# Handing ScalarE's exps lasting buffers, and raising the floor of TensorE work in the attention ramp

## The chip, the core and the metric

The kernel runs on one core of a Trainium2 chip. Its engines have queues of their own, each executed in order: TensorE (PE in the profile, its weight loads PEld), VectorE (DVE), ScalarE (ACT), GpSimd (POOL) and SyncE (SP, which here only issues DMAs). They are tied together by semaphores. The metric is the device time of one execution in microseconds; before the change it is 1373.56 us, the median of three runs (1373.54, 1373.56 and 1381.38).

## What is computed

Two pairs of layers act on x, 2048 rows of 512 values. The first layer of a pair is a spectral filter: layer norm, two-dimensional real FFT, product with a complex filter, inverse FFT, added to x. The second is attention with 32 query heads of 16 channels and one key and value head that all of them share.

```python
def _A_ref(x, w_r, w_i):
    X = rfft2(x.astype(float32), axes=(-2, -1))
    X = X * (w_r + 1j * w_i)
    return irfft2(X, s=(S, D), axes=(-2, -1)).astype(bfloat16)

def _B_ref(x, wq, wk, wv, wo):              # H = 32, Dh = 16
    q = (x @ wq).reshape(B, S, H, Dh).transpose(0, 2, 1, 3)
    k, v = x @ wk, x @ wv
    scores = einsum("bhqd,bkd->bhqk", q, k) * (Dh ** -0.5)
    p = softmax(scores, axis=-1)
    o = einsum("bhqk,bkd->bhqd", p, v)
    return o.transpose(0, 2, 1, 3).reshape(B, S, H * Dh) @ wo

x = x + _A_ref(_layernorm(x), w_r, w_i)
x = x + _B_ref(_layernorm(x), wq, wk, wv, wo)
x = x + _A_ref(_layernorm(x), w_r, w_i)
x = x + _B_ref(_layernorm(x), wq, wk, wv, wo)
```

## The kernel before

The Fourier transforms are matrix products on TensorE with butterflies on VectorE around them; x stays in SBUF for the whole kernel. The attention of a layer is cut into 32 blocks (four groups of 512 queries, four groups of eight heads, two parities), each of 16 key chunks by four heads. The unit of work is one head, one key chunk of 128 keys and 512 queries: a score matmul that uses 32 rows of the array (L1212, four of them side by side), an exponential, and a matmul with V that uses 32 columns (L1234).

The exponentials are shared out between two paths. ScalarE takes two units in one instruction (`exp`, L1217), from one of the two PSUM slots `sa` to a bf16 tile `e2`. VectorE takes one unit in one instruction (`p1`, L1224), which computes an approximation by way of the bit pattern; three shifted copies of it are summed in the matmul with V, two of them made by GpSimd (L1228) or VectorE. Over both layers ScalarE has 1252 such instructions and VectorE 1592.

The order on every engine is written out beforehand, by a planner in Python (`Plan`) that runs while the program is built. It keeps a clock for each engine and a price for each operation (an exp 908 ns, a `p1` 600 ns, a round of matmuls 220 ns), picks step by step what could start first and emits the instruction. The chip follows these orders without change; only the waits between engines decide when a thing starts. Three of the planner's rules matter here:

- `live` and `bufs` (L158, L159): at most `E_BUFS = 8` exps may hold a tile whose matmuls with V are not yet emitted. `do_pv` (L537) counts the readers of a tile down and lowers `live` at the last.
- `fill` (L437): before TensorE takes something up, dummy matmuls on zeros (`dummy`, L939; its two forms are at L941 and L945) are put in while the columns streamed in the last `WIN = 3413` ns are fewer than `warm`. Where the gap is too short for a dummy, it is put in all the same, ahead of the useful work, if they are fewer than `force`.
- The ramp (L439): for 20,000 ns from the point where VectorE joins the attention (`dve_on`, set when the last values of V are evacuated by L1190), `fill` uses `RAMP_WARM` and `RAMP_FORCE` in place of `WARM` and `FORCE`.

The `e2` tiles come from a tile pool with 13 buffers (`t2`, L930). Four kinds of data live there: an exp's result, the transposed x at the front of a spectral layer (`tr_evac`, L998, read by `mm1`, L1006), and the inverse transform's result and its sums (`inv_evac`, L1115, and `radix_v`, L1120). A new tile takes a buffer when all accesses to the previous one are over: the instruction that writes first waits for the engines that read and for the engine that wrote. For an exp these are TensorE (readers) and ScalarE itself (writer), beside TensorE again for the scores.

Of the kernel before, what the change touches and what calls it, by code (L numbers as in the profile page):

```python
# [8 lines left out]
ACT = mybir.ActivationFunctionType  # L9
ALU = mybir.AluOpType  # L10
P = 128
BF = mybir.dt.bfloat16
# [6 lines left out]
NC = 4  # L19
# [3 lines left out]
SCALE = DH ** -0.5  # L23
# [37 lines left out]
def radix4(nc, sd, x, half, o, piece):  # L61

    s, d = sd[:, 0], sd[:, 1]
    tt = nc.vector.tensor_tensor
    if piece == 0:
        tt(out=s, in0=x[:, 0:2, :], in1=x[:, 2:4, :], op=ALU.add)
    elif piece == 1:
        tt(out=d, in0=x[:, 0:2, :], in1=x[:, 2:4, :], op=ALU.subtract)
    elif piece == 2:
        tt(out=o[:, 0, :], in0=s[:, 0, :], in1=s[:, 1, :], op=ALU.add)  # L70
        tt(out=o[:, 2, :], in0=s[:, 0, :], in1=s[:, 1, :], op=ALU.subtract)
    else:
        o = o.rearrange("p j (i f) -> p (j i) f", i=2)
        a, b = (d[:, i].rearrange("p (i f) -> p i f", i=2) for i in range(2))
        tt(out=o[:, 2:8:5], in0=a, in1=b[:, ::-1], op=ALU.subtract)
        tt(out=o[:, 6:2:-3], in0=a, in1=b[:, ::-1], op=ALU.add)
# [34 lines left out]
class Plan:  # L111
# [17 lines left out]
    WARM = 3500.0  # L129
    FORCE = 3150.0  # L130
    RAMP = 20000.0
    RAMP_WARM = 4200.0
    RAMP_FORCE = 3900.0
    HOLD = 200.0
    NB = 4
    TIER = 500.0
# [400 lines left out]
    def do_pv(self, start, sel):  # L537
        self.fill(start, "col")
        at = self.at
        start = max(start, self.t["PE"] + (0.0 if self.mode == "col" else self.PE_SW))  # L540
        end = start + self.MM
        for s in sel:
            e = next(x for x in self.pv if x[1:5] == s[1:5] and x[5] is s[5] and x[6:8] == s[6:8])
            self.pv.remove(e)
            _, _, b, h, kc, tile, j, p, ref = e
            if b not in self.acc_of:
                self.acc_of[b] = self.grab("b", "acc")
            first = (b, h) not in at.begun
            at.begun.add((b, h))
            stop = self.made(b, h) and not any(x[2] == b and x[3] == h for x in self.pv)  # L550
            self.em.pv(self.acc_of[b], h, kc, tile, j, p, first, stop)
            ref[0] -= 1
            if ref[0] == 0:
                self.live[ref[1]] -= 1
            if self.made(b) and not any(x[2] == b for x in self.pv):
                at.done(b, self.acc_of.pop(b), end)
        self.mode = "col"
        self.hist.append((start, 128.0 * len(sel)))
        self.t["PE"] = end
# [99 lines left out]
class Layer:  # L659
# [11 lines left out]
    def __init__(self, plan, em, first, last):  # L671
        self.plan, self.em, self.first, self.last = plan, em, first, last
        self.next = None
        self.at = Attn(plan, em, self)
        self.rs = {}
        self.Pk, self.G, self.FT, self.W, self.Dz, self.IT, self.UT, self.V, self.sb, self.xn = ({} for _ in range(10))
        self.mm1_done = {}
        self.g_done = {}
        self.stat = {}
        self.gate = []  # L680
        self.sd_of = {}
# [194 lines left out]
class Emit:  # L876


    def __init__(self, ctx, tc, ins, out):
        nc = self.nc = tc.nc  # L880
        A_x, self.w_r, self.w_i, B_wq, B_wk, B_wv, B_wo = ins
        mk = lambda nm, b=1, **kw: ctx.enter_context(tc.tile_pool(name=nm, bufs=b, **kw))
        const = mk("const")
        psum = mk("psum", space=bass.MemoryType.PSUM)
        self.pool = mk("work")
        self.sa = [psum.tile([P, 2, 512], F32, name=f"sa{i}") for i in range(2)]
        self.b = [psum.tile([P, 512], F32, name=f"b{i}") for i in range(Plan.NB)]
        nc.scalar.preload_act_table_set("natural_log_exp_and_others")
        self.x = const.tile([P, R, T, 512], BF, name="x_sb")
        xv = A_x.flatten_outer_dims().rearrange("(r p t) d -> p r t d", r=R, p=P, t=T)  # L890
        ht = host_tables()
        self.dram = {k: nc.inline_tensor(v, name=f"const_{k}").ap() for k, v in ht.items()}
        tabs = {name: const.tile(list(ht[name].shape), BF, name=f"tab_{name}") for name in ("ident", "PH", "PS")}
        self.ident, self.PH, self.PS = tabs["ident"], tabs["PH"], tabs["PS"]
        nc.sync.dma_start(out=self.x[:, :, 0], in_=xv[:, :, 0])
        nc.scalar.dma_start(out=self.ident, in_=self.dram["ident"])
        nc.scalar.dma_start(out=self.PH, in_=self.dram["PH"])
        for t in range(1, T):
            nc.sync.dma_start(out=self.x[:, :, t], in_=xv[:, :, t])
        self.wq = const.tile([P, NC, D], BF, name="wq")  # L900
        self.wk = const.tile([P, NC, DH], BF, name="wk")
        self.wk8 = const.tile([P, NC, P], BF, name="wk8")
        self.part = const.tile([P, 2], F32, name="part")
        self.wv = const.tile([P, NC, DH], BF, name="wv")
        self.WO = const.tile([P, 4, D], BF, name="WO")
        self.eps = const.tile([P, 1], F32, name="eps")
        self.zero = const.tile([P, 512], BF, name="zero")
        self.KA = const.tile([P, S], BF, name="KA")
        self.KB = const.tile([P, S], BF, name="KB")
        self.warm = const.tile([P, 2, 16], U16, name="warm")  # L910
        nc.vector.memset(self.zero, 0.0)
        nc.vector.memset(self.eps, EPS)
        nc.gpsimd.memset(self.warm, 0)
        self.key = const.tile([P, 1], F32, name="key")
        self.pw = phase_weights()
        self.VS = [const.tile([P, NT, 32], BF, name=f"vs{i}") for i in range(1 + K_PH)]
        for i, v in enumerate(self.VS):
            nc.gpsimd.memset(v, 1.0 if i == 0 else self.pw[i - 1])
        nc.gpsimd.int64_add(self.warm[:, 1].bitcast(U64), self.warm[:, 0].bitcast(U64), 0)
        half = (np.arange(P)[:, None] // DH % 2 == np.arange(2)).astype(np.float32)  # L920
        self.w_dma = [(self.PS, self.dram["PS"]), (self.wq, B_wq.rearrange("(c p) j -> p c j", p=P)),
                      (self.wk, B_wk.rearrange("(c p) j -> p c j", p=P)), (self.wv, B_wv.rearrange("(c p) j -> p c j", p=P)),
                      (self.part, nc.inline_tensor(half, name="const_part").ap()),
                      (self.WO, B_wo.rearrange("(g p) c -> p g c", p=P))]
        self.out_v = out.flatten_outer_dims().rearrange("(r p t) d -> p r t d", r=R, p=P, t=T)
# [1 line left out]
    def t4(self, shape, dt=BF, tag="w4", bufs=17):  # L927
        return self.pool.tile([P] + list(shape), dt, name=tag, tag=tag, bufs=bufs)

    def t2(self, shape, dt=BF, bufs=13):  # L930
        return self.pool.tile([P] + list(shape), dt, name="e2", tag="e2", bufs=bufs)

    def small(self, shape, name, bufs=6):
        return self.pool.tile([P] + list(shape), F32, name=name, tag=name, bufs=bufs)
# [63 lines left out]
    def tr_evac(self, L, tiles, slot, eng):  # L998
        xt = self.t2([2, NC, P])
        src = self.ps(slot).bitcast(BF)  # L1000
        dst = xt.rearrange("p i c x -> p (i c x)")
        self.copy(eng, dst, src)
        L.xt = dict(getattr(L, "xt", {}))
        L.xt[tuple(tiles)] = xt

    def mm1(self, L, tiles, i, slot, cc):  # L1006
        xt = L.xt[tuple(tiles)]
        self.nc.tensor.matmul(self.ps(slot), lhsT=xt[:, i, cc, :], rhs=self.PH[:, cc, :], start=(cc == 0), stop=(cc == NC - 1),
                              skip_group_check=True)

    def mm1_evac(self, L, x, slot):
        t, r = x
# [102 lines left out]
    def inv_evac(self, L, t, b, j, slot, eng):  # L1115
        if (t, b) not in L.V:
            L.V[(t, b)] = self.t2([4, 256])
        self.copy(eng, L.V[(t, b)][:, 2 * j:2 * j + 2, :].rearrange("p a b -> p (a b)"), self.ps(slot))

    def radix_v(self, L, t, b, piece):  # L1120
        if t not in L.UT:
            L.UT[t] = self.t4([2, R, 256])
        if piece == 0:
            L.sd_of[(t, b)] = self.t2([2, 2, 256])
        u = L.UT[t][:, b]
        radix4(self.nc, L.sd_of[(t, b)], L.V[(t, b)], 128, u, piece)

    def y_mm(self, L, t, r, slot, s, n):
        if s == 4:
# [20 lines left out]
            self.nc.tensor.transpose(ps[:, cc, i, :], xn[:, cc * P:(cc + 1) * P], self.ident)  # L1150

    def copy(self, eng, out, in_):
        if eng == "ACT":
            self.nc.scalar.copy(out=out, in_=in_)
        else:
            self.nc.vector.tensor_copy(out=out, in_=in_)

    def trn_evac(self, L, t, j, slot, eng):
        xT = L.at.xT
# [54 lines left out]

    def exp(self, slot, us):
        e = self.t2([2, 512])
        self.nc.scalar.activation(out=e, in_=self.ps(slot), func=ACT.Exp, scale=SCALE)  # L1217
        return e

    def new_t(self):  # L1220
# [131 lines left out]
```

The softmax here doesn't subtract the row's maximum and nothing guards it: scores larger than these inputs give would overflow.

## Time and profile before

| | |
|---|---|
| median of the runs | 1373.56 us (1373.54 to 1381.38) |
| profiled execution | 1376.24 us |
| its span | 1374.4 us |
| mean granted TensorE clock | 0.991 |
| weight loads (PEld) busy | 432.2 us, 13009 instructions |
| matmuls | 12937 |
| exps (L1217) | 1252 |
| dummies at L941, L945 | 55 and 44 matmuls (the latter are four to a dummy) |

A profile row "start, duration, engine, line, operation" gives microseconds from the start of the span. A matmul's duration includes its passage through the array, so four matmuls side by side that take 0.39 us each follow the previous four after 0.22 us. ScalarE's instructions overlap too: an exp of 1.02 us can start 0.904 us after the one before. A share of busy time close to 100% says that an engine is nearly always occupied, not that it works at its peak. The clock granted to TensorE is given as a share of full speed; it changes only in steps of 3.41 us. Instructions that only wait on a semaphore (EVENT_SEMAPHORE) do not count as busy.

### The profile page before, as it was taken

How to read it: one execution, taken by the hardware profiler on the slowest of the kernel's cores; microseconds unless marked ns; L12 is line 12 of the kernel's file. 1: busy time of each engine (PE TensorE's matmuls, PEld its weight loads, DVE VectorE, ACT ScalarE, POOL GpSimd, SP SyncE). 2: the span in 40 equal slices, each digit the busy share in tenths (PEclk: the TensorE clock that was granted, in tenths of full speed). 3: DMA queues.
4: the chain of work that ended last, by engine and by line, in shares of the span. 5: the costliest groups of instructions: out<-in, count | busy, mean ns of one | idle time of the engine just before them, and what ended most of it. 6: DMA issues, size and time to landing. Idle time of an engine off the chain costs nothing.

```text
span 1374.4 us, 32527 instructions
## 1 busy us (share of the span) xinstructions
PE 1331.3 (97%) x12937; PEld 432.2 (31%) x13009; DVE 1288.9 (94%) x2286; ACT 1253.5 (91%) x1408; POOL 828.0 (60%) x810
## 2 busy tenths in 40 slices
PE   9999999999999999999999999999999999999998
PEld 5632222222223222232246322222222222222222
DVE  6985899999999999999979879999999999998998
ACT  6498899999998999999954989999999989997996
POOL 0001677757776777657720027777777767776775
PEclk9998899999999999999999999999999999999999
DMA  8100000000000000000051000000000000000000
GB/s 285 40 1 1 2 1 2 1 2 1 2 2 1 2 2 1 2 2 1 2 161 40 1 1 2 2 2 9 9 2 1 5 13 2 1 2 17 1 2 17
DMA packets 21081, 22.07 MB, mean 16 GB/s; under 512 B 2240, under 2 KB 19648, under 8 KB 20928
## 3 DMA queue, kind: packets, MB, share of 16 engines
q1 hardware_dynamic: 20640, 19.44, 4.5%
q8 instruction: 101, 1.65, 0.5%
q14 instruction: 52, 0.43, 0.1%
q10 hardware_dynamic: 288, 0.56, 0.1%
HBM read 17.89 MB, written 2.10 MB: 15 GB/s over the span
## 4 chain that ended last, share of the span: by engine, by line
PE 61%; DVE 17%; ACT 15%; issue 4%; DMA 1%; SPq 1%; POOL 1%; DVEq 0%; POOLq 0%; ACTq 0%
PE sa_65 L1212 8%; PE sa_64 L1212 8%; PE b_68 L1234 7%; PE b_69 L1234 7%; PE b_67 L1234 7%; PE b_66 L1234 5%; PE b_68 L1212 3%; PE b_69 L1212 2%; PE b_66 L1212 2%; PE b_67 L1212 2%; DVE st L959 1%; DVE x_sb L1144 1%; DVE xd L57 1%; DMA w_368<-const_FT 1%; PE b_68 L1133 1%
## 5 line engine op out<-in xcount | busy, mean ns | idle before, releaser
L1212 PEld LDWEIGHTS <-KA 32*128 32x128 bf16 x2048 | 82.7, 91 | 226.9 <-issue 220.9
L1212 PEld LDWEIGHTS <-KB 32*128 32x128 bf16 x2048 | 79.7, 91 | 234.0 <-issue 229.8
L1234 PEld LDWEIGHTS <-vs_96 128*32 128x32 bf16 x2504 | 104.2, 94 | 108.4 <-issue 99.7
L1234 PEld LDWEIGHTS <-vs_97 128*32 128x32 bf16 x1592 | 93.7, 94 | 72.1 <-issue 69.4
L1234 PEld LDWEIGHTS <-vs_98 128*32 128x32 bf16 x1592 | 71.0, 94 | 83.4 <-issue 77.8
L1234 PEld LDWEIGHTS <-vs_99 128*32 128x32 bf16 x1592 | 70.3, 94 | 78.6 <-issue 73.0
L1228 POOL INT64_ADD w_1549<-w_1548 x1 | 1.0, 1042 | 123.8 <-DVE w_1548 L1224 123.8
L1228 POOL INT64_ADD w_11726<-w_11725 x1 | 1.0, 1040 | 111.8 <-DVE w_11725 L1224 111.8
L959 DVE BATCH_NORM_STATS2 st<-x_sb 128x6 f32<-128x512 bf16 x52 | 35.6, 685 | 4.7 <-DMA x_sb<-in_A_x_dram 3.9
L1099 PEld LDWEIGHTS <-xd 128*128 128x128 bf16 x256 | 24.0, 98 | 9.3 <-DVE xd L57 4.4
L1252 DVE TENSOR_TENSOR on<-raw,rc 128x512 bf16<-128x512 f32 x32 | 21.8, 682 | 0.1
L1212 PE MATMUL sa_65<-w_903,KB 32*128 32x512 bf16 x86 | 18.2, 387 | 0.3
L1212 PE MATMUL sa_65<-w_11080,KB 32*128 32x512 bf16 x86 | 18.0, 382 | 0.3
L1212 PE MATMUL sa_64<-w_903,KA 32*128 32x512 bf16 x84 | 17.1, 392 | 1.1 <-ACT e_2850 L1217 0.2
L1212 PE MATMUL sa_65<-w_903,KA 32*128 32x512 bf16 x84 | 17.6, 394 | 0.5 <-ACT e_2505 L1217 0.2
L1212 PE MATMUL sa_64<-w_11080,KA 32*128 32x512 bf16 x84 | 16.6, 382 | 1.3 <-ACT e_13213 L1217 0.4
L1212 PE MATMUL sa_65<-w_2548,KB 32*128 32x512 bf16 x80 | 17.1, 382 | 0.9 <-ACT e_4970 L1217 0.2
L1212 PE MATMUL sa_64<-w_903,KB 32*128 32x512 bf16 x86 | 17.5, 396 | 0.3 <-ACT e_2605 L1217 0.2
L1212 PE MATMUL sa_65<-w_11080,KA 32*128 32x512 bf16 x84 | 17.1, 383 | 0.5 <-ACT e_12682 L1217 0.2
L1212 PE MATMUL sa_64<-w_11080,KB 32*128 32x512 bf16 x86 | 16.9, 383 | 0.4 <-ACT e_12782 L1217 0.2
L1212 PE MATMUL sa_65<-w_4927,KB 32*128 32x512 bf16 x80 | 16.9, 382 | 0.4 <-ACT e_6743 L1217 0.2
L1212 PE MATMUL sa_65<-w_12725,KB 32*128 32x512 bf16 x78 | 16.4, 381 | 0.4
(6372 smaller groups left out, 6569.3 us busy)
## 6 DMA issues: line engine op xcount, KB each, us to landing
it<-const_IT SPq DMA_DIRECT2D x8, 640.0 KB, 6.3
x_sb<-in_A_x_dram SPq DMA_DIRECT2D x4, 512.0 KB, 7.2
out_dram<-x_sb SPq DMA_DIRECT2D x16, 128.0 KB, 1.8
tab_PH<-const_PH ACTq DMA_DIRECT2D x1, 512.0 KB, 5.3
w_107<-const_FT SPq DMA_DIRECT2D x1, 512.0 KB, 8.9
w_112<-const_FT SPq DMA_DIRECT2D x1, 512.0 KB, 8.4
tab_PS<-const_PS SPq DMA_DIRECT2D x1, 512.0 KB, 7.8
wq<-in_B_wq_dram SPq DMA_DIRECT2D x1, 512.0 KB, 7.9
```

Of the source, the lines that this page charges most:

```text
L57: nc.vector.tensor_tensor(out=sd[:, 2 * piece:2 * piece + 2, :], in0=x[:, 0:2, :], in1=x[:, 2:4, :], op=ALU.subtract if piece else ALU.add)
L959: self.nc.vector.bn_stats(st, self.ps(slot) if slot else self.x[:, x[1], x[0], :])
L1099: self.nc.tensor.matmul(ps[:, k, :], lhsT=z, rhs=L.IT[t][:, u, w:w + 256], start=(a == 0 and i == 0), stop=(a == 1 and i == 1), skip_group ...
L1133: self.nc.tensor.matmul(self.ps(slot), lhsT=L.UT[t][:, b, r, 128 * i:128 * i + 128], rhs=self.PS[:, s, :], start=(s == 0), stop=(s == n - ...
L1144: self.nc.vector.tensor_tensor(out=x, in0=self.ps(slot), in1=x, op=ALU.add)
L1212: self.nc.tensor.matmul(o, lhsT=KX[rs, kc * P:(kc + 1) * P], rhs=at.QT[qb][rs, g, :], start=True, stop=True, skip_group_check=True)
L1228: self.nc.gpsimd.int64_add(t[p][:, 0:n].bitcast(U64), t[0][:, 0:n].bitcast(U64), DELTA[p] * FOUR)
L1234: self.nc.tensor.matmul(self.ps(slot)[32 * h:32 * h + 32, :], lhsT=V[:, kc, :], rhs=rhs, start=first, stop=last, skip_group_check=True)
L1252: self.nc.vector.tensor_tensor(out=on.rearrange("p a h d -> p h a d"), in0=raw[:, :, :, 0:16], in1=rc.unsqueeze(3).to_broadcast([P, 2, 16, ...
```

## The change

The 13 `e2` buffers become tiles that last for the whole kernel (`e2_0` to `e2_12`). `t2` hands out the oldest idle one; `free2` puts it back when the planner has emitted its last reader. `wrote` remembers for each buffer which engine last wrote it, and with which instruction; when the same engine writes it again by way of `wrote`, the dependence between these two writes is declared void. This holds for exps and for the transposed x. Buffers written for the inverse transform have their record dropped. `copy` now returns its instruction. Beside this, two of the planner's numbers are raised, `RAMP_WARM` from 4200 to 4800 and `RAMP_FORCE` from 3900 to 4300.

```diff
-    RAMP_WARM = 4200.0
-    RAMP_FORCE = 3900.0
+    RAMP_WARM = 4800.0
+    RAMP_FORCE = 4300.0
...
             if ref[0] == 0:
                 self.live[ref[1]] -= 1
+                if ref[1] == "ACT":
+                    self.em.free2(tile)
...
+        self.tc = tc
+        self.e2 = [const.tile([P, 1024], BF, name=f"e2_{i}") for i in range(13)]
+        self.idle, self.home, self.writer = list(range(13)), {}, {}
...
-    def t2(self, shape, dt=BF, bufs=13):
-        return self.pool.tile([P] + list(shape), dt, name="e2", tag="e2", bufs=bufs)
+    def t2(self, shape):
+
+
+        home = self.idle.pop(0)
+        dims = " ".join("abc"[:len(shape)])
+        view = self.e2[home].rearrange(f"p ({dims}) -> p {dims}", **dict(zip("abc", shape)))
+        self.home[id(view)] = (home, view)
+        return view
+
+    def free2(self, view):
+        self.idle.append(self.home.pop(id(view))[0])
+
+    def wrote(self, eng, view, i):
+
+
+        home = self.home[id(view)][0]
+        last = self.writer.get(home)
+        if last is not None and last[0] == eng:
+            self.tc.declare_no_dep(i.ins, last[1].ins, reason="the readers of that write waited for it")
+        self.writer[home] = (eng, i)
...
-        self.copy(eng, dst, src)
-        L.xt = dict(getattr(L, "xt", {}))
-        L.xt[tuple(tiles)] = xt
+        self.wrote(eng, xt, self.copy(eng, dst, src))
+        L.xt[tuple(tiles)] = [xt, 2 * NC]
...
+        L.xt[tuple(tiles)][1] -= 1
+        if L.xt[tuple(tiles)][1] == 0:
+            self.free2(L.xt.pop(tuple(tiles))[0])
...
         self.copy(eng, L.V[(t, b)][:, 2 * j:2 * j + 2, :].rearrange("p a b -> p (a b)"), self.ps(slot))
+        self.writer.pop(self.home[id(L.V[(t, b)])][0], None)
...
+            self.writer.pop(self.home[id(L.sd_of[(t, b)])][0], None)
...
+        if piece == 1:
+            self.free2(L.V[(t, b)])
+        if piece == 3:
+            self.free2(L.sd_of[(t, b)])
...
         e = self.t2([2, 512])
-        self.nc.scalar.activation(out=e, in_=self.ps(slot), func=ACT.Exp, scale=SCALE)
+        self.wrote("ACT", e, self.nc.scalar.activation(out=e, in_=self.ps(slot), func=ACT.Exp, scale=SCALE))
         return e
```

## The prediction

> **What bounds the kernel now.** I read the page's shares first, then the chain of work that ended last, then busy time by stretches, and then single instructions. The first two lines below are from part 1 and part 2 of the page, the third from part 4.
>
> ```profile
> PE 1331.3 (97%) x12937; PEld 432.2 (31%) x13009; DVE 1288.9 (94%) x2286; ACT 1253.5 (91%) x1408; POOL 828.0 (60%) x810
> ...
> PEclk9998899999999999999999999999999999999999
> ...
> PE 61%; DVE 17%; ACT 15%; issue 4%; DMA 1%; SPq 1%; POOL 1%; DVEq 0%; POOLq 0%; ACTq 0%
> ```
>
> Three engines are almost full, and no single one is the bound: the chain lies mostly on PE and changes over to DVE and ACT for stretches. The two long attention stretches, in busy time (columns: stretch, length, busy of PE, weight loads, DVE, ACT, POOL with instruction counts, granted clock, DMA):
>
> ```profile
> 172.00:640.00 468.00, 459.11 (x4690) 134.19 (x4715) 461.21 (x790) 455.29 (x498) 337.58 (x330) 1.00 0.01 2
> 840.00:1240.00 400.00, 392.78 (x4043) 111.66 (x4057) 394.64 (x657) 391.40 (x421) 301.25 (x290) 1.00 0.01 4
> ```
>
> There PE, DVE and ACT are each at 97 to 99%. A saving on one of them alone is worth little; it counts only where the chain passes through it. The row of granted clock above shows an 8 in the fourth and fifth slices, so I looked at those in the steps in which the clock record changes, 3.41 us:
>
> ```profile
> 122.01:125.42 3.41, 2.49 (x19) 0.78 (x18) 2.60 (x7) 3.38 (x4) 0.00 (x0) 1.00 0.02 5
> 125.42:128.83 3.41, 3.41 (x23) 0.59 (x21) 1.29 (x2) 2.10 (x3) 2.06 (x2) 0.50 0.00 0
> ...
> 135.66:139.07 3.41, 3.41 (x18) 0.64 (x17) 1.98 (x3) 0.68 (x2) 2.06 (x2) 0.50 0.00 0
> ...
> 811.50:814.91 3.41, 2.93 (x28) 0.80 (x21) 2.22 (x4) 2.54 (x4) 2.31 (x3) 1.00 0.02 7
> 814.91:818.33 3.42, 2.74 (x17) 0.74 (x17) 2.99 (x5) 2.91 (x3) 1.86 (x3) 1.00 0.00 0
> ...
> 1238.17:1241.58 3.41, 3.34 (x9) 0.81 (x9) 2.00 (x4) 1.64 (x2) 1.05 (x2) 0.50 0.11 38
> ```
>
> From 125.4 to 145.9 TensorE ran five of six such steps at half clock, just after VectorE's share of the attention begins (the "ramp" of the planner). The ramp of the second layer, 811 to 818, is the same planned work and kept the full clock. So the two are a measured pair. The last values' evacuation (L1190) opens the ramp, the second block's evacuation (L1241) closes it, in the timeline of VectorE:
>
> ```profile
> 122.05 0.23 DVE L1190 CAST vs_96<-b_69 128x64 bf16<-128x64 f32 x1
> ...
> 146.86 0.71 DVE L1241 STREAM_TRANSPOSE raw<-b_66 128x512 f32<-128x512 f32 x1
> ```
>
> ```profile
> 806.42 0.22 DVE L1190 CAST vs_96<-b_66 128x64 bf16<-128x64 f32 x1
> ...
> 824.94 0.70 DVE L1241 STREAM_TRANSPOSE raw<-b_67 128x512 f32<-128x512 f32 x1
> ```
>
> 24.8 us against 18.5 us: the half clock cost 6.3 us in the first layer and nothing in the second.
>
> **The change part by part.** *The wait on ScalarE's own write.* The instructions of the exp's line begin with
>
> ```profile
> L1217 ACTq EVENT_SEMAPHORE  x1116: 17/17/17, 84.9 to 1362.6; - x186
> ```
>
> Of 1252 exps, 1116 have a separate wait instruction ahead of them: the exp itself waits on ScalarE's semaphore and the event instruction on TensorE's. By the wait values of the program the own write waited for lies 10 to 15 ScalarE instructions back, some 10 us, so that wait is never the late one; what it costs is that the wait for the scores needs an instruction of its own. Without one (the timeline's first pair) and with one (the second), the exp follows its scores like this:
>
> ```profile
> 75.91 0.39 PE L1212 MATMUL sa_65<-w_903,KA 32*128 32x512 bf16 x2
> ...
> 76.33 1.02 ACT L1217 ACTIVATE e_954<-sa_65 128x1024 bf16<-128x1024 f32 x1
> ```
>
> ```profile
> 432.86 0.39 PE L1212 MATMUL sa_65<-w_4927,KB 32*128 32x512 bf16 x2
> ...
> 433.35 1.02 ACT L1217 ACTIVATE e_6266<-sa_65 128x1024 bf16<-128x1024 f32 x1 [4.73 <-PE sa_64 L1212]
> ```
>
> That is 0.03 us after the matmul's end without, 0.10 us with. Pairing every exp with the semaphore update of its scores gives medians of 0.023 (40 late exps) and 0.083 us (180), so 0.06 us for each exp whose scores come late. An exp that is not late gains nothing: back to back, exps start every 0.904 us with the event instruction and without. Late (scores at least 0.84 us after the previous exp's start) are 280 exps with an event instruction: 280 x 0.06 = 16.8 us is the ceiling. The floor is what the chain of waits shows: it passes from PE to ACT 12 times between 172 and 640 and 15 times between 840 and 1240, so 27 x 0.06 = 1.6 us, and a few more outside. Other chains lie close behind the shown one (PE at 98%), so I take the value near the floor: -2.0 us. It could also be zero, if each saved 0.06 us ends in a wait for DVE.
>
> *The lasting buffers.* 13 buffers before, 13 after, of the same size; the exp still waits for TensorE's last read of its buffer, in the same instruction as for its scores. The planner holds at most 8 exps at a time, so there is normally an idle one. Buffers of the transposed input, of V and of its sums come from the same 13 and have their writer forgotten, so a few dozen exps keep extra waits. No instruction is added. Zero; what hides it is that the oldest idle buffer is handed out. If none but a just-freed buffer were there, an exp would wait for a round of L1234 (0.22 us); the tight places (602 to 606 us, where x is transposed into these buffers) have a few such, under 1 us.
>
> *RAMP_WARM 4200 to 4800, RAMP_FORCE 3900 to 4300.* The planner puts dummy matmuls (L941, L945) into the ramp until that many columns lie in its window of 3413 ns, and forces them ahead of useful work below the second number. A ramp has 22 us, or 6.5 windows. The rise of 600 columns is 600/512 x 6.5 = 8 more dummies in a ramp, of which 400/512 x 6.5 = 5 are forced. Before, each ramp had 13. At full clock dummies start 0.22 us apart (6.34, 6.56, 6.77 us in the trace), so forced ones cost at most 1.1 us a ramp; PE has 0.5 to 0.7 us idle in each of the steps at 811 to 818 above, so I take half: +1.1 us for both ramps. What it may bring is the 6.3 us of the first ramp, all or nothing.
>
> [...] The step at 811 with 28 matmuls kept its clock, the one at 122 with 19 lost it; eight dummies over 6.5 windows, more at the thin ones, make up that order of difference. [...]
>
> *Sum.* -5.2 - 2.0 = -7.2 us, so 1376.24 - 7.2 = 1369.0 for the profiled execution. Its span is 1374.4 with 1.8 us around it, and it is 2.7 us above the median of the runs (1373.56). The half-clock stretch at 1238 to 1245 may be that difference: ScalarE stands idle for 5.1 us at its end, waiting for scores. I leave it as it is on both sides. Against the median: 1366.4 us.
>
> **The rivals.** *The clock is not won (0.18).* The first ramp still falls under what the clock wants. For it: I can't see the limit, only pairs of rows, and the thin time is in the waits of TensorE for VectorE, where the plan and the chip differ. Against: the second ramp is clear with today's dummies. 1373.6 - 2.0 + 1.1 to 2.0 (dummies at half clock start 0.43 us apart, as 3.30 and 3.72 us show) = 1373.
>
> *The wait is worth more (0.14).* ACT at 97% in the long stretches may be the pacing engine oftener than one chain shows. Two thirds of the ceiling, 11 us, with the ramp: 1373.6 - 5.2 - 11 = 1357.
>
> *The clock is lost in another place (0.16, the slower side).* The second ramp kept its clock with steps of PE busy 2.74 and 2.93 us, barely more than the 2.49 that lost it, and the stretch at 1238 lost it. Moving everything by some microseconds moves the thin stretches against the steps of the clock. If the second ramp is caught and the first is not saved: +6.3 + 2.0 - 2.0 = 1380. It decides once one 3.41 us step of the second ramp holds as little as the first's. More dummies there speak against; the run of 1381.38 among three of before speaks for such a loss being possible.
>
> *It doesn't do what it says.* If the event instructions stay (the readers' wait and the scores' wait not merged), only the ramp acts: 1368. This is inside the first case's spread.
>
> **How the numbers follow.** First case 0.52, 1366.4, own range 1361 to 1371; then 0.18 at 1373, 0.14 at 1357, 0.16 at 1380. The range 1355 to 1379 leaves out about half of the slower rival and the far tails. One per cent is 13.7 us, about what a measurement of this kernel tells from no change: faster than 1359.8 takes most of the third case and a little of the first, 0.16; slower than 1387.3 needs two lost ramps and more, 0.05; within it 0.79.
>
> **What would show it.** The event instructions at the exp's line fall from 1116 to well under 200, and late exps start about 0.03 us after their scores. The steps between 122 and 146 us show a clock of 1.00, and the first layer's pair of lines comes to about 18.5 us. More than 13 dummies lie in each ramp, and the second ramp is under 1 us longer. The prediction is wrong if 0.50 rows stay in the first ramp or appear in the second, or if the long stretches (172 to 640 in particular) get shorter by more than 3 us or longer by any.

## The result, and the profile after

The changed kernel takes 1359.87 us in the median of four runs (1359.69 to 1365.84), the kernel before beside it 1373.55 us (1372.03 to 1381.38): a ratio of 0.990, 95% interval 0.9854 to 0.9946. The prediction was 1366.4 us with a range of 1355 to 1379. Direction and range hold; the gain is 13.7 us where 7.2 were forecast. In a second set, five runs against 17 of before, the ratio is 0.9903 (0.9874 to 0.9932).

Every run lists its mean granted TensorE clock, and the time goes with it. In what follows "at full clock" means a mean of 0.999 or 1.000. Two executions in all (1423 us and 1631 us) had a mean clock of 0.84 and 0.65, for a reason that no run here shows, and are left out of the comparisons.

The changed kernel's page, the lines that answer to those of before (busy shares, clock row, the chain that ended last):

```profile
PE 1316.5 (97%) x12952; PEld 426.1 (31%) x13022; DVE 1283.2 (95%) x2285; ACT 1249.4 (92%) x1409; POOL 825.7 (61%) x809
...
PEclk9999999999999999999999999999999999999999
...
PE 40%; ACT 39%; DVE 16%; issue 2%; POOL 1%; DMA 1%; SPq 1%; DVEq 0%; POOLq 0%; ACTq 0%
```

The shares have hardly moved. The clock row has lost both its 8s. The chain has changed: ScalarE holds 39% of it where it held 15%. The first ramp of the changed kernel, in the steps of its own clock record (columns as before: stretch, length, PE, weight loads, DVE, ACT, POOL, clock, DMA):

```profile
120.89:124.30 3.41, 2.97 (x34) 1.23 (x32) 2.06 (x6) 3.28 (x5) 0.00 (x0) 1.00 0.02 5
124.30:127.72 3.42, 2.86 (x27) 0.74 (x23) 2.45 (x4) 2.93 (x4) 0.65 (x1) 1.00 0.00 0
127.72:131.13 3.41, 3.17 (x34) 0.64 (x26) 2.67 (x5) 2.34 (x4) 2.65 (x4) 1.00 0.00 0
131.13:134.54 3.41, 2.62 (x26) 0.82 (x26) 2.43 (x4) 2.85 (x3) 1.10 (x2) 1.00 0.00 0
```

The clock stays at 1.00. The same pair of lines as before, the last values' evacuation (now L1218) and the second block's (now L1269), in VectorE's timeline:

```profile
122.28 0.22 DVE L1218 CAST vs_109<-b_69 128x64 bf16<-128x64 f32 x1
...
141.88 0.70 DVE L1269 STREAM_TRANSPOSE raw<-b_66 128x512 f32<-128x512 f32 x1
```

19.6 us instead of 24.8. The same pair in the second layer:

```profile
796.05 0.22 DVE L1218 CAST vs_109<-b_66 128x64 bf16<-128x64 f32 x1
...
815.65 0.70 DVE L1269 STREAM_TRANSPOSE raw<-b_67 128x512 f32<-128x512 f32 x1
```

Here it is 19.6 us instead of 18.5, with the full clock on both sides. So the first ramp gained by the clock, and the second, where no clock had been lost, became 1.1 us longer. The exps now wait for their scores themselves, as two lines of the timeline show:

```profile
446.79 0.39 PE L1240 MATMUL sa_64<-w_4622,KA 32*128 32x512 bf16 x2
...
447.22 1.02 ACT L1245 ACTIVATE e_1_87<-sa_64 128x1024 bf16<-128x1024 f32 x1
```

The exp starts 0.04 us after the matmul ends (446.79 + 0.39 = 447.18), where it was 0.10 with a wait instruction between. Over the whole trace, 6 exps have a wait instruction (1116 before), and late exps start 0.023 us (median) after their scores' semaphore. Back to back, exps start 0.904 us apart, as before.

### The profile page after: what moved, and what is told of

It reads as the page before. It is cut to its first block, busy times and chain, and to the rows that moved or that the text cites. A ratio compares the mean times of both kernels' runs of the same rounds, so it can differ in the third digit from the quotient of the medians.

```text
span 1357.7 us, 31441 instructions
## 1 busy us (share of the span) xinstructions
PE 1316.5 (97%) x12952; PEld 426.1 (31%) x13022; DVE 1283.2 (95%) x2285; ACT 1249.4 (92%) x1409; POOL 825.7 (61%) x809
## 4 chain that ended last, share of the span: by engine, by line
PE 40%; ACT 39%; DVE 16%; issue 2%; POOL 1%; DMA 1%; SPq 1%; DVEq 0%; POOLq 0%; ACTq 0%
PE sa_64 L1240 5%; PE sa_65 L1240 5%; PE b_67 L1262 5%; PE b_68 L1262 5%; PE b_69 L1262 4%; ACT e_10_96 L1245 3%; ACT e_3_89 L1245 3%; ACT e_0_86 L1245 3%; ACT e_2_88 L1245 3%; ACT e_11_97 L1245 3%; ACT e_9_95 L1245 3%; ACT e_12_98 L1245 3%; ACT e_5_91 L1245 3%; ACT e_7_93 L1245 3%; ACT e_1_87 L1245 3%; ACT e_6_92 L1245 3%
## 5 line engine op out<-in xcount | busy, mean ns | idle before, releaser
L1240 PEld LDWEIGHTS <-KA 32*128 32x128 bf16 x2048 | 77.6, 91 | 220.4 <-issue 215.5
L1245 ACT ACTIVATE e_0_86<-sa_65 128x1024 bf16<-128x1024 f32 x50 | 52.2, 1043 | 7.0 <-PE sa_64 L1240 6.2
L1245 ACT ACTIVATE e_2_88<-sa_65 128x1024 bf16<-128x1024 f32 x51 | 53.0, 1039 | 1.8 <-PE sa_64 L1240 0.8
L1245 ACT ACTIVATE e_8_94<-sa_64 128x1024 bf16<-128x1024 f32 x49 | 51.2, 1044 | 2.9 <-PE sa_64 L1240 2.4
L1245 ACT ACTIVATE e_10_96<-sa_64 128x1024 bf16<-128x1024 f32 x49 | 51.0, 1040 | 3.1 <-PE sa_65 L1240 3.0
L1245 ACT ACTIVATE e_9_95<-sa_64 128x1024 bf16<-128x1024 f32 x50 | 52.0, 1040 | 0.8 <-PE b_68 L1240 0.7
L1245 ACT ACTIVATE e_4_90<-sa_65 128x1024 bf16<-128x1024 f32 x50 | 52.2, 1044 | 0.3
L1245 ACT ACTIVATE e_8_94<-sa_65 128x1024 bf16<-128x1024 f32 x49 | 51.4, 1049 | 1.1 <-PE sa_64 L1240 1.1
L1245 ACT ACTIVATE e_7_93<-sa_64 128x1024 bf16<-128x1024 f32 x49 | 51.4, 1048 | 0.9 <-PE sa_65 L1240 0.8
L1245 ACT ACTIVATE e_6_92<-sa_65 128x1024 bf16<-128x1024 f32 x48 | 50.1, 1043 | 2.1 <-PE sa_64 L1240 2.1
L1245 ACT ACTIVATE e_2_88<-sa_64 128x1024 bf16<-128x1024 f32 x47 | 48.9, 1039 | 3.3 <-PE sa_64 L1240 3.3
L1245 ACT ACTIVATE e_12_98<-sa_65 128x1024 bf16<-128x1024 f32 x49 | 51.1, 1043 | 0.7 <-PE b_67 L1240 0.4
L1245 ACT ACTIVATE e_12_98<-sa_64 128x1024 bf16<-128x1024 f32 x47 | 49.3, 1048 | 2.5 <-PE sa_65 L1240 2.1
L1245 ACT ACTIVATE e_0_86<-sa_64 128x1024 bf16<-128x1024 f32 x49 | 51.3, 1047 | 0.2
L1245 ACT ACTIVATE e_10_96<-sa_65 128x1024 bf16<-128x1024 f32 x48 | 50.4, 1050 | 0.9 <-PE sa_65 L1240 0.7
```

Source lines behind the costliest of these rows:

```text
L1240: self.nc.tensor.matmul(o, lhsT=KX[rs, kc * P:(kc + 1) * P], rhs=at.QT[qb][rs, g, :], start=True, stop=True, skip_group_check=True)
L1245: self.wrote("ACT", e, self.nc.scalar.activation(out=e, in_=self.ps(slot), func=ACT.Exp, scale=SCALE))
```

## The experiments

Three parts were to be told apart: the wait, the lasting buffers, and the two ramp numbers; the latter may act through the clock or through the order that the planner writes.

**The ramp numbers alone.** The kernel before with

```diff
-    RAMP_WARM = 4200.0
-    RAMP_FORCE = 3900.0
+    RAMP_WARM = 4800.0
+    RAMP_FORCE = 4300.0
```

> The kernel before with the two ramp numbers alone (4800 and 4300). If the clock in the first ramp is all that these numbers buy, as the prediction has it: 5 to 6 us below before, no step at half clock between 122 and 146 us, the pair of lines L1190 to second L1241 near 18.5 us, 1116 or so wait instructions still there. If the ramp numbers also make a better schedule of the rest: 10 us or more below before. If they did nothing and the whole gain is the wait: within 1 us of before.

Measured: 1366.58 us, ratio 0.9935 (0.9911 to 0.9959), 7.9 us below before (1374.51 in that set). Of the comparable runs two were at clock 1.000 (1365.0 and 1365.4) and the others at 0.998 or 0.999, up to 1366.9. The profiled one had no half clock in the first ramp, took 19.6 us for each ramp's pair of lines, and lost the clock for 3.4 us at 1230. More than the expected 5 to 6 us, so the clock is not all that the numbers buy.

**The wait alone.** The changed kernel with the ramp numbers of before:

```diff
-    RAMP_WARM = 4800.0
-    RAMP_FORCE = 4300.0
+    RAMP_WARM = 4200.0
+    RAMP_FORCE = 3900.0
```

> The changed kernel with the two ramp numbers put back to 4200 and 3900. If only the passages from PE to ACT on the shown chain count (the prediction): 2 us below before. If ScalarE paces the long stretches oftener than one chain shows: 6 to 11 us below before, spread evenly over both long stretches. The half clock in the first ramp should be seen again; if it is gone here too, it was a matter of the ramp's timing against the clock's steps and not of the number of dummies.

Measured: 1368.71 us, ratio 0.9940 (0.9907 to 0.9974), 5.8 us below before. Every engine's order is that of before, so blocks can be compared one by one. From the second to the thirtieth block's evacuation it takes 517.2 us (before 519.7), from the 34th to the 54th 359.0 us (360.5). The gain is spread over both long stretches, 2.5 and 1.4 us. The chain of this run:

```profile
PE 49%; ACT 33%; DVE 14%; issue 2%; DMA 1%; SPq 1%; POOL 0%; DVEq 0%; POOLq 0%; ACTq 0%
```

Without the wait ScalarE holds 33% of the chain, and with the ramp numbers alone 19%, so the shift is the wait's doing and not the ramp's. In this profiled run the half clock in the first ramp is there again, as the stretch shows:

```profile
122.00:146.00 24.00, 22.72 (x125) 4.28 (x123) 13.44 (x25) 12.97 (x14) 8.21 (x8) 0.57 0.00 1
```

It also lost the clock in the second ramp, from 807.3 to 810.7 us, where the profile of before, with the same order, had kept it. But three of its seven runs kept the clock (0.999 or 1.000), and those took 1362.0 to 1362.2 us. Losing the ramp's clock differs from run to run; it is not a fixed property of an order. At equal mean clock (0.985, 0.991 and 0.992) the four other runs lie 4.8 to 5.6 us below the runs of before.

**The lasting buffers alone.** The changed kernel, ramp numbers and buffers included, with the declaration left out:

```diff
         if last is not None and last[0] == eng:
-            self.tc.declare_no_dep(i.ins, last[1].ins, reason="the readers of that write waited for it")
+            pass
```

> The changed kernel, lasting buffers and ramp numbers as changed, but the dependence on ScalarE's own last write kept. If the lasting buffers cost and bring nothing by themselves: the same time as the ramp numbers alone, within 1 us, with over 1100 wait instructions back. If it is the order in which buffers are handed out that matters: near the changed kernel's 1360 us.

Measured: 1366.80 us (0.9947, 0.9925 to 0.9968); at clock 1.000, 1364.5 to 1365.5 us, the same as the ramp numbers alone. 1113 wait instructions are back and late exps again start 0.083 us after their scores. Lasting buffers bring nothing and cost nothing by themselves; they are what lets the declaration be made. The profiled run lost the clock in the second ramp, 802 to 816 us, which the profile of before had not shown.

**Half of the waits.** The changed kernel with the declaration for the six odd buffers only:

```diff
-        if last is not None and last[0] == eng:
+        if last is not None and last[0] == eng and home % 2:
```

> The changed kernel with the wait on the own last write kept for the seven even buffers and voided for the six odd ones, so that about half of the wait instructions are back; the order on every engine is that of the changed kernel. If every late exp passes its 0.06 us on, wherever it lies, the undisturbed time lies half way between the changed kernel (1359.7) and the ramp numbers alone (1365.0): about 1362.4. If only a few places on one chain pay, it lies at one end or the other, within 1 us.

The exps' line has

```profile
L1245 ACTq EVENT_SEMAPHORE  x611: 17/17/17, 85.2 to 1348.6; - x153
```

Measured: median 1367.21 us of 12 runs (0.9940, 0.9916 to 0.9964); the five at full clock took 1361.9 to 1363.8 us, their middle 1362.8. 611 of 1113 waits are 55%, and 55% of the way from 1359.8 to 1365.2 is 1362.8. So about half of the waits cost about half of the time. The other seven had clocks of 0.985 to 0.994: in the changed kernel's own order on every engine the clock is lost in many runs.

**Ramp numbers 4600 and 4100.** The changed kernel with

```diff
-    RAMP_WARM = 4800.0
-    RAMP_FORCE = 4300.0
+    RAMP_WARM = 4600.0
+    RAMP_FORCE = 4100.0
```

> The changed kernel with ramp numbers 4600 and 4100. Theory 1, each added dummy costs a little: fewer dummies, so 0.2 to 1 us below the changed kernel's 1359.7 when the clock holds, but the half clock comes back in some runs. Theory 2, the numbers only tip the planner's choices and the rest of the order changes by chance: the undisturbed time goes with the length of the order as planned, which is 2 us shorter than the changed kernel's, so about 1357.5.

Measured: 1364.27 us (0.9936, 0.9914 to 0.9958). None of 12 runs kept the full clock; the six best were at 0.994 or 0.995, 1361.5 to 1363.2 us. The profiled one was at half clock from 125 to 139, and its pair of lines to the second block ends at 146.1 us against 141.9 in the changed kernel. Taking these 4.2 us off the 1361.8 of that run gives an estimate of 1357.6 for this order at full clock, which is what theory 2 says; it wasn't seen directly. Theory 1 would have it at 1358.7 to 1359.5.

**Ramp numbers 5400 and 4900.** The same two lines with these values.

> The changed kernel with ramp numbers 5400 and 4900, 26 more dummies. Theory 1, forced dummies at 0.22 us each, half of them on the path: about 3 us above 1359.7, no half clock anywhere in the ramps. Theory 2, the order as planned is 11 us longer: about 1370, no half clock either.

Measured: 1371.65 us (0.9979, 0.9960 to 0.9997). At clock 0.999 or 1.000, 1369.9 to 1371.8 us. The ramps kept their clock in the profiled run, which lost it elsewhere, at 594 to 604 us. Theory 2: the order as planned is 11 us longer, and so is the time. The 26 more dummies would be 5.7 us at 0.22 us each. In the ramps the pair of lines took 21.6 us each time, 2.0 us more than in the changed kernel; the rest of the loss lies elsewhere, in the order that the planner wrote.

**True prices for the planner.** The changed kernel with

```diff
-    PE_LAT = {"ACT": 252.0, "DVE": 205.0, "POOL": 252.0}
+    PE_LAT = {"ACT": 192.0, "DVE": 205.0, "POOL": 252.0}
...
-    ACT_EXP = 908.0
+    ACT_EXP = 904.0
```

> The changed kernel with the planner's prices brought to what the traces show: an exp 904 ns instead of 908, and from scores to exp 192 ns instead of 252, the 60 ns that the wait instruction took. If the planner gains from true prices: 1357 to 1358 (its order is 1.7 us shorter). If its order differs only by chance: anywhere from 1355 to 1366, and no better where the thin stretches lose the clock.

Measured: 1364.31 us (0.9943, 0.9918 to 0.9969), at full clock 1363.5 to 1365.5 us. It is slower than the changed kernel although its order is 1.7 us shorter by the planner's clock. A miss: truer prices made a plan that the chip falls behind by more. Why is open.

**The changed kernel again.** No edit.

> The changed kernel as it is, in more runs, since a median of four may be a lucky draw: the kernel with half of the waits has the same order and held the full clock in 5 of 12 runs. If the changed kernel keeps the clock by itself: nearly all runs within 0.5 us of 1359.7. If it is the same draw as for that order: about half of the runs at 1359.7, the others 1 to 8 us above with a clock of 0.985 to 0.998, and a median of 1360 to 1365.

Measured: five comparable runs, 1359.6, 1360.0, 1360.1, 1361.5 and 1365.0 us, the first four at 0.999 or 1.000. With the four of the first measurement that is seven of nine at full clock, with a median of 1360.0. The half-waits kernel, with the same order, had five of twelve. So the first median was no lucky draw, but the clock isn't safe in this order.

**Force 4000.** The changed kernel with

```diff
-    RAMP_WARM = 4800.0
-    RAMP_FORCE = 4300.0
+    RAMP_WARM = 4400.0
+    RAMP_FORCE = 4000.0
```

> The changed kernel with ramp numbers 4400 and 4000. By the planner's own books the first number changes nothing here (every gap in a ramp is too short for a dummy that would wait its turn); the second alone sets the order. This order is 2.4 us shorter than the changed kernel's, and its thinnest 3413 ns of the ramps hold 3107 columns against 2816. If the undisturbed time goes with the length of the order: 1357.4. If the clock goes with the thinnest stretch: more runs undisturbed than the changed kernel has; if it doesn't, as few or fewer.

Measured: 1358.15 us, ratio to before 0.9890 (0.9863 to 0.9917). Four of six runs kept the full clock, at 1357.7 to 1358.3 us; the others had 0.995 and 0.997 (1363.3 and 1361.5). At full clock this is 1.8 us below the changed kernel; 2.4 were expected from the length of the order. The clock was not kept oftener (four of six runs, seven of nine for the changed kernel), so nothing here says that the thinnest stretch of the plan sets the odds. It is the fastest version of this study; the runs of this and of the changed kernel in the same set (medians 1358.15 and 1360.1) overlap, so only the comparison at full clock tells them apart.

**No dummies in the first ramp.** The changed kernel's order with the dummies of one ramp not emitted; they compute nothing that is used.

```diff
-            self.em.dummy(where, fresh, mode)
+            if not (ramp and start < 300000.0):
+                self.em.dummy(where, fresh, mode)
```

> The changed kernel in its own order, with the 17 dummies of the first ramp left out (they compute nothing) and those of the second kept. If the dummies hold the clock: the first ramp runs at half clock in every run, 4 to 7 us above the changed kernel, and the second does not. If the dummies are only a burden on TensorE and the clock is kept by the order of the work: up to 3.7 us (17 x 0.22) below 1359.7.

Measured: 1366.89 us (0.9956, 0.9935 to 0.9976), and in all 12 runs a clock of 0.993 or less. Three steps of the clock record in its first ramp, before and after the fall:

```profile
121.00:124.41 3.41, 2.37 (x31) 0.95 (x28) 2.79 (x8) 3.33 (x5) 0.00 (x0) 1.00 0.02 5
124.41:127.82 3.41, 3.11 (x18) 0.53 (x17) 2.69 (x5) 2.97 (x4) 1.88 (x2) 0.50 0.00 0
127.82:131.24 3.42, 3.42 (x22) 0.65 (x18) 2.81 (x5) 2.87 (x4) 2.01 (x3) 0.50 0.00 0
```

It stays at 0.50 until 151.7 us, 27 us in a row; the second ramp with its dummies stays at full clock. The dummies are what holds the clock, shown in one order with nothing else changed. The profiled run, with no other loss of the clock, is 5.9 us above the changed kernel. TensorE is busy for 3.42 of 3.42 us in the last of these steps, at half clock: the busy share says nothing of it.

## Why the prediction was right, and where its sum was not

At full clock the wait alone takes 1362.1, the changed kernel 1359.8, the ramp numbers alone 1365.2 (its two runs at 1.000). So the wait is worth 5.4 us (1365.2 to 1359.8) and the ramps' new order 2.3 us (1362.1 to 1359.8). From these, before at full clock would be 1367.5, an estimate: no run of before reached it (its best, 1369.6, had 0.997). A straight line through the runs of before beside the experiments, 0.9 us for each 0.001 of the clock, comes to 1367.2. The median of before, 1373.6, lies 6.1 us above, lost to the clock; the changed kernel's median lies 0.1 us above its own. So 5.4, 2.3 and 6.0 make up the 13.7; they are differences that must add up, and the straight line and the equal-clock comparison of the second experiment are what supports them.

- *The clock of the first ramp, -6.3 forecast, about 6.0 found.* The 6.0 is all that the median run of before lost to the clock, wherever it lost it; in its profiled run most of that was the first ramp. The -6.3 and the +1.1 of the dummies make the -5.2 of the sum. The reason given was right: thin work. The row is 121.00 to 124.41 of the kernel without dummies: TensorE was busy for 2.37 of 3.41 us, and the next step ran at half clock. In the profile of before the step from 122.01, after which the clock was lost too, had TensorE busy for 2.49 us with no idle gap longer than 0.48 us: the idle time lay in short pieces. The last section counts the work. Two things were not foreseen. The loss is settled in each run anew, so the change moved the odds (no full-clock run of before among 30 in one set, seven of nine after) rather than curing it. The numbers are not alone in this: with them by themselves all five runs had 0.998 or more, but with the wait gone and the old numbers three of seven kept the full clock too. And the two ramps of before were no safe pair: the same order also lost the clock of the second ramp, in the profiled run of the second experiment.
- *The wait, -2.0 forecast, -5.4 found.* The term was mis-sized, at the choice of an end of its span. The mechanism held: 0.06 us for each late exp, nothing for those that follow back to back. The value was taken near the floor of 1.6 us, which counts the passages from PE to ACT on one chain; the runs give a third of the ceiling of 16.8 us. The chain follows one path back, and with PE, DVE and ACT at 97 to 99% others lie just behind it. What the runs showed instead is that the cost is spread: half of the waits cost half, and both long stretches gain. That ScalarE moves from 15% of the chain to 33% without the wait agrees, but is weaker evidence: on the chain of before some 190 pieces called "issue" stand between two instructions of ScalarE, after it three, so part of the shift may be how a chain is followed through a wait instruction. Which late exps pay was not isolated.
- *The dummies, +1.1 forecast, -2.3 found.* The step that failed is the count and what it costs. Eight more dummies in a ramp were forecast. By their weight loads, 17 stand in each ramp where 14 stood (the 13 of the prediction counts matmul records, of which one is missing). Only three more, yet the second ramp's pair of lines took 1.1 us longer at full clock, twice the share of a ramp in the forecast, and the first's came to the same 19.6 us. If each ramp lost 1.1 us, the rest of the kernel gained about 4.5 (an estimate, from 2.3 + 2.2). `RAMP_WARM` does nothing here: with the second number held at 3900 or at 4000, the planner, run by itself, writes the same order for 4200, 4400, 4600 and 5000. `RAMP_FORCE` alone acts, and its effect is mostly that the greedy planner makes other choices for the rest of the kernel. The lengths it planned were 1347.5, 1349.9, 1351.4 and 1361.2 us for 4000, 4300, 3900 and 4900, in no order; the times at full clock follow them: 1358.0, 1359.8, 1362.1 and about 1370.5. A gain of 2.3 us from the new order is chance, and 5400 and 4900 show that it could as well have been a loss of 8.
- *The lasting buffers, 0 forecast.* Right: 1364.5 to 1365.5 with them, 1365.0 and 1365.4 without.
- *The rivals.* "The wait is worth more" was right in direction with half its size (5.4 against 11 us). "The clock is lost in another place" does happen, run by run: the second ramp at 802 to 816 in the third experiment, 1230 in the first. It did not decide the median. Of the prediction's own tests, those on the wait instructions (6 left) and on the clock between 122 and 146 us held. The second ramp grew by 1.1 us where less than 1 was named, and the first pair came to 19.6 us and not 18.5. The test that no long stretch gets shorter by more than 3 us failed: from the second to the thirtieth block the changed kernel takes 513.7 us against 519.7, of which the wait gives 2.5 (517.2 with it alone in the order of before) and the new order 3.5.

## What to carry to other kernels

Where an instruction waits both on its own engine and on another, look whether the first wait can ever be the late one; if not, dropping it may save the separate wait instruction: here 1116 became 6, at 0.06 us for each instruction whose data came late and nothing for the rest. With three engines at 97% or more, the passages on one chain gave only a lower bound of the saving here (1.6 us against 5.4): a spread cost is better tested by restoring half of it. And when a generated order and a clock that is lost in some runs only both move with a constant, judge each at full clock, by its own order, before calling the constant better.

## What the runs showed of the hardware that was not expected

The clock is lost at different places in different runs of one program: before ranges over 1369.6 to 1381.7 us in 30 runs, with mean clocks of 0.997 to 0.985, and each 0.001 of the clock goes with about 0.9 us. The order without dummies in the first ramp kept the full clock in none of 12 runs. With 17 there the changed kernel kept it in seven of nine runs, the same order with half of the waits in five of twelve; with 14, the wait alone kept it in three of seven.

The traces show what goes with a loss. In the profile of before the clock record changes at 125.42, 128.83, 132.25, 145.90, 1238.16 and 1244.99 us, each a whole number of steps of 3.41 us from the others, and this grid lies elsewhere in other runs: a step begins at 122.01 in the profile of before, at 121.21 in that of the wait alone (the same order), at 120.89 in that of the changed kernel. For each step the columns that its matmuls stream can be counted, with a matmul on 32 rows or 32 columns as a quarter, as the planner's window does (each spread over 0.22 us, at half clock 0.43). In the profile of before three steps at full clock were followed by one at half clock, those from 128.83, 1234.75 and 122.01; they hold about 2630, 2810 and 3010 columns. Of its steps at full clock that were followed by another the thinnest hold about 3030 and 3040, and in the profile of the changed kernel, whose record shows 1.00 from 4.84 to 1356.52 us, 3030 and 3040 too. In the eleven profiles, all but that of 1631 us and with the ends of the span left out, 14 steps were followed by one at half clock, with about 1830 to 3140 columns; of those that kept the clock two hold about 2790 and 2890, all others 3030 or more. The two groups overlap, so these counts show no sharp limit. Busy time and the number of matmuls separate them less: the step from 1234.75 of before had TensorE busy for 3.27 us with 17 matmuls and lost the clock (2810 columns), the step from 814.91 of before had 2.74 us with 17 and kept it (3490), and the step from 131.13 of the changed kernel 2.62 us with 26 and kept it (3480).

This also shows how narrow the prediction's pair of ramps was: the step from 122.01 held about 3010 columns and lost the clock, the one from 804.67 about 3030 and kept it. And the changed kernel is not safe, as an estimate from its trace: a step that began there between 121.3 and 122.0 would hold 2560 to 2930 columns, fewer than the thinnest step in which this profile kept the clock, and its grid, with steps from 120.89 and 124.30, missed that. That the position of the grid decides in the other runs too is likely but not shown, as only profiled runs show theirs.
